# First batch of a fused attention and expert kernel: order of scores and z turns, place of the weight loads, issuer of the tail stores

## The chip, the cores and the metric

The kernel runs on one core of one Trainium2 chip. The metric is the device time of one execution in microseconds (us). The time before is the median of six executions, 1219.36 us, with 1209.82 as the shortest and 1236.12 as the longest.

## The reference

There are 8 batches of 3008 rows. Per batch, with z of 64 columns and u and v of 256:

```
scores = (1/S) * z @ z.T              # 3008 x 3008
attn   = maximum(scores, 0) ** 2
x      = u * (attn @ v)               # 3008 x 256
h      = x @ w_in                     # 256 -> 2048
out    = (h * sigmoid(1.702 * h)) @ w_out   # 2048 -> 256
```

Inputs and output are f32; the kernel works in f16 with f32 sums.

## The kernel before, in words

**Chunks and units.** A batch is cut into six chunks of 512 queries (the last has 448). A chunk has 24 key blocks of 128, and two key blocks make a *unit* (i, jp): two score matmuls of 64 rows (L216), a Relu on ScalarE (`rl`, L228), and a square on VectorE (`a`, L242). Scores are symmetric, so a chunk computes only the units on and behind its diagonal. Units whose key blocks lie in a later chunk are also turned by a DMA transpose from SP's queue (`tt<-a`, L248), and that later chunk multiplies by the turned copy. In batch 0 there are 20 such transposes.

**Attend.** `attend(b, i)` (L270) gives a list of steps for chunk i. A step is one or two matmuls of `V16` with a unit (`o`, L301). In batch 0, chunks 0 and 1 use 128-row matmuls, the later ones 64-row pairs. When a chunk's sum is complete, VectorE multiplies it with the turned u (`xt`, L318). For the 64-row pairs, a nop on POOL stands between the two halves (`post`, L82): it waits for TensorE to reach step 23, and later POOL instructions stand behind it.

**Order.** All engines run in the order in which the program is written; each engine takes its instructions strictly in that order. Tables place the rest of the work by chunk and step: SCHED0 (L570) says at which step how many units are scored (`take`, L581), TURN0 and LOAD0 when u is turned and the next u is loaded, FIRST_ZT (L569) when a chunk of z is turned in chunk 0, LOADW (L566) when W2 is loaded.

**Start of batch 0.** z comes in f32 by DMA. `first_cast(g)` (L120) makes two f16 copies of a 512-row piece on VectorE; `first_zt(g)` (L125) turns the piece with four TensorE transposes into a PSUM tile `zp` and copies it to `ZT` (L134 on ScalarE for piece 0, L136 on VectorE for the others). The copy reads PSUM in order and writes f16 values 8 bytes apart, since a row's four key blocks lie side by side. Warm-up matmuls on zeros (L94) fill TensorE before. In the kernel before, all six pieces are cast ahead of the first three units' squares on VectorE:

```
    warm_up(9)
    first_cast(0); first_zt(0); first_cast(1); first_zt(1)
    for g in range(2, NCH):
        first_cast(g)
    take(0, 2); take(0, 1); load_u(0, 1); first_zt(2); warm_up(2)
```

(written here on fewer lines than in the code). Pieces 3 to 5 are turned at steps 3, 11 and 19 of chunk 0.

**Weights.** W1 (four DMAs, L636) and W2 (four DMAs, L372) are f32 in memory and f16 on the chip, and are loaded from POOL's queue, as u is (L186). W1's first half is issued after chunk 0, its second half after chunk 1, each behind a small copy (`hold`) that waits for that chunk's `xt`. W2 follows in chunk 4. Four VectorE sums over W2 (`weight_sums`, L374) give the right-hand sides of a seven-product scheme.

**Up and down.** `up_group` (L335) computes one 128-column pair of h: four matmuls (`hg`, L342), Gelu on ScalarE (`gf`, L350), a scaling on VectorE (`gt`, L351). The first 20 groups of a batch are laid into chunk 5's steps, one behind each other two or three `o` matmuls; the other 28 alternate with the products of chunks 0 to 3 (`st`, L432). After a chunk's eighth group, each later group carries one more VectorE sum (`left_sum`, L395). The last two chunks go through `down64` (L495), whose matmuls alternate with the first scores of the next batch; it too has POOL nops, at its steps 16 and 32. At its end `store` (L476) issues the output DMA from ScalarE's queue.

Of the kernel before, what the change touches and what calls it, by code (L numbers as in the profile page):

```python
# [11 lines left out]
P = 128  # L12
# [3 lines left out]
def kernel(  # L16
# [75 lines left out]
    def warm_up(n):  # L92

        w = ps1.tile([P, CH], F32, name="w", tag="ps1")  # L94
        for k in range(n):
            pe.matmul(w, nil[:, :P], nil, start=(k == 0), stop=(k == n - 1))
# [23 lines left out]
    def first_cast(g):  # L120
        m = g % CB * CB
        for c in range(2):
            dve.tensor_copy(ZT["st"][g // CB][:, m:m + CB, c, :], ZT["f"][g // CB][:, m:m + CB, :])  # L123

    def first_zt(g):  # L125
        z2 = ZT["st"][g // CB][:, g % CB * CB:(g % CB + 1) * CB]
        zp = ps1.tile([P, CB, P], F16, name="zp", tag="ps1")
        for k in range(CB):
            pe.transpose(zp[:, k, :], z2[:, k, :, :], ident)
        zt = ZT[0][:, g * CB:(g + 1) * CB, :].rearrange("d n p -> d (n p)")  # L130
        nb = CB if g < NCH - 1 else CB - 1
        dst = zt[:, :nb * P].rearrange("d (p n) -> d n p", n=nb)
        if g == 0:
            act.activation(dst, zp[:, :nb, :], AF.Copy, scale=1.0)  # L134
        else:
            dve.tensor_copy(dst, zp[:, :nb, :])  # L136
        if nb < CB:
            dve.tensor_copy(zt[:, nb * P:], zp[:, nb, :])

# [130 lines left out]
    def attend(b, i, both=False):  # L270


        n = width(i)
        js, cs = list(range(NJ - 1)), range(2)
        own = i * CB
        if b == 0 and i == 3:
            js = js[own:-CB + 1] + js[:own] + js[-CB + 1:]
        elif b and i == NCH - 3:
            js = js[own:own + 2] + js[own + CB:-CB + 1] + js[:own] + js[own + 2:own + CB] + js[-CB + 1:]
        elif b and i < NCH - 2:  # L280
            js = js[own:own + 2] + js[own + CB:-CB + 1] + js[own + 2:own + CB] + js[:own] + js[-CB + 1:]
        half = [(0, TOP, NJ - 1), (1, LOW, NJ - 1)]
        if both:
            order = [[(c, FULL, j)] for j in js[:-CB] for c in cs] + [[(c, FULL, j)] for c in cs for j in js[-CB:]]
            order.insert(-CB, half)
        elif i == NCH - 1:
            order = [half] + [[(c, FULL, j)] for c in cs for j in js]
        else:
            order = [[(0, TOP, j), (1, LOW, j)] for j in js] + [half] + [[(1, TOP, j), (0, LOW, j)] for j in js]
        flat = [(k, m) for k, ms in enumerate(order) for m in ms]  # L290
        first = {c: next(m for m in flat if m[1][0] == c) for c in cs}
        final = {c: [m for m in flat if m[1][0] == c][-1] for c in cs}
        acc, turn = {}, NJ if order[-1][0][1] != FULL else -1

        def step(k):
            done = []
            for m in order[k]:
                c, h, j = m
                if (k, m) == first[c]:
                    acc[c] = ps1.tile([P, CH], F32, name="o", tag="ps1")  # L300
                ins = pe.matmul(  # L301
                    acc[c][:, :n], V16[b][h, j, c, :], weights(b, i, j)[h],
                    start=(k, m) == first[c], stop=(k, m) == final[c],
                )
                if k == turn:
                    behind(acc["sig"], ins)
                done.append(ins)
            if k == turn - 1:
                acc["sig"] = post(done)
            for c in cs:  # L310
                if k == final[c][0]:
                    gate(c)

        def gate(c):
            ut = UT[b, i][:, c].rearrange("p q t -> p (q t)")
            x = XT[b, i]
            if i < NCH - 1 or b % 2:
                dve.tensor_tensor(x[:, c, :n], acc[c][:, :n], ut[:, :n], ALU.mult)  # L318
            else:
                dve.tensor_tensor(x[:, c, :LFULL], acc[c][:, :LFULL], ut[:, :LFULL], ALU.mult)  # L320
                dve.tensor_tensor(XT[b + 1, i][:, c, LAST:], acc[c][:, LFULL:n], ut[:, LFULL:n], ALU.mult)

        XT[b, i] = XT.get((b, i)) or pa.tile([P, NCC, CH], F16, name="xt", tag="xt", bufs=6)
        if i == NCH - 1 and b % 2 == 0:
            XT[b + 1, i] = pa.tile([P, NCC, CH], F16, name="xo", tag="xo")
        return [lambda k=k: step(k) for k in range(len(order))]
# [38 lines left out]
    LO, HI = slice(0, NFF // 2), slice(NFF // 2, NFF)  # L365
    C0, C1 = slice(0, P), slice(P, D)

    def load_w2(k):
        hold = const.tile([P, 1], F16, name=f"hold2{k}")
        pool.tensor_copy(hold, XT[0, NCH - 3][:, 0, :1])  # L370
        fs = slice(k * CB, (k + 1) * CB)
        pool.dma_start(W2[:, fs], moe_w_out.rearrange("(fo p) c -> p fo c", p=P)[:, fs])  # L372

    def weight_sums():  # L374
        b11, b12, b21, b22 = W2[:, LO, C0], W2[:, LO, C1], W2[:, HI, C0], W2[:, HI, C1]
# [119 lines left out]
    def down64(b, k):  # L495

        ns = blocks(b)[k][1] // P
        shift, per = (2, 2) if ns == CB else (1, 1)
        order = [(s, (s + shift) % ns, ff) for s in range(ns) for ff in range(NFF)]
        turns = [32] if ns == CB else [16, 32]  # L500
        last = {s // per: n for n, o in enumerate(order) for s in o[:2]}
        yp, sigs = {}, {}

        def step(n):
            s0, s1, ff = order[n]
            done = []
            for s, h in ((s1, LOW), (s0, TOP)):
                new = s // per not in yp
                if new:
                    yp[s // per] = ps1.tile([P, 2, D], F32, name="yp", tag="ps1")  # L510
                ins = pe.matmul(  # L511
                    yp[s // per][:, s % per, :], GT[b, k, ff // CB][h, ff % CB, s * P:(s + 1) * P], W2[h, ff, :],
                    start=new, stop=n == last[s // per],
                )
                if n in turns:
                    behind(sigs[n], ins)
                done.append(ins)
            if n + 1 in turns:
                sigs[n + 1] = post(done)
            for m in yp:  # L520
                if n == last[m]:
                    if (b, k) not in Y:
                        Y[b, k] = pw.tile([P, CB, D], F32, name="y", tag="y")
                    act.activation(Y[b, k][:, m * per:(m + 1) * per, :], yp[m][:, :per, :], AF.Copy, scale=1.0 / FSC)  # L524
            if n == len(order) - 1:
                store(b, k, ns - 1)

        return turns, [lambda n=n: step(n) for n in range(len(order))]

# [33 lines left out]
    TURN0 = {(i, (38, 28)[i] if i < 2 else NJ + 4 if i < NCH - 1 else 12): i for i in range(NCH)}  # L563
    LOAD0 = {(i, n): i + 2 for i, n in TURN0 if i + 2 < NCH}
    TURN = {(1, NJ + 4): 2, (2, NJ + 4): 3, (4, NJ + 4): 4, (5, 8): 5}
    LOADW = {4: 0, 10: 1, NJ + 3: 2, NJ + 9: 3}  # L566
    LOAD = {(3, NJ + 4): 4, (4, NJ + 5): 5}

    FIRST_ZT = {3: 3, 11: 4, 19: NCH - 1}  # L569
# [22 lines left out]
    first_z((0, CB, 2 * CB, 4 * CB, NJ))  # L592
    for n0 in range(VB, NJ, VB):
        load_v(0, n0, sp)
    warm_up(9)
    first_cast(0)
    first_zt(0)
    first_cast(1)
    first_zt(1)
    for g in range(2, NCH):  # L600
        first_cast(g)
    take(0, 2)
    take(0, 1)
    load_u(0, 1)
    first_zt(2)
    warm_up(2)

    for b in range(B):
        nup = NCH * NFG
# [2 lines left out]
        for i in range(NCH):  # L612
            for n, step in enumerate(attend(b, i, b == 0 and i < 2)):
                if b == 0 and i == 0 and n == 5:
                    load_u(0, 0)
                if b == 0 and i == 0 and n in FIRST_ZT:
                    first_zt(FIRST_ZT[n])
                if (i, n) in turn:
                    turn_u(b, turn[i, n])
                if (i, n) in load:  # L620
                    load_u(b, load[i, n])
                if b == 0 and i == NCH - 2 and n in LOADW:
                    load_w2(LOADW[n])
                take(b, sched[i].get(n, 0))
                if i == NCH - 1 and n >= HEAD and (n - HEAD) * LAGY // (2 * NJ - 2 - HEAD) >= head and head < LAGY:
                    up_group(b, head)
                    head += 1
                    if b == 0 and head in (1, 3, 5, 7):
                        weight_sums()[head // 2]()
                step()  # L630
            if b == 0 and i < 2:
                hold = const.tile([P, 1], F16, name=f"hold{i}")
                pool.tensor_copy(hold, XT[b, i][:, 0, :1])
                w1v = moe_w_in.rearrange("(q k c) f -> q c k f", k=NCC, c=QW)
                for k in range(2 * i, 2 * i + 2):
                    pool.dma_start(W1[k * QW:(k + 1) * QW], w1v[k])  # L636
        more = b + 1 < B
        if more:
            for i in range(2):
# [55 lines left out]
```

## Time and profile before

| quantity | value |
|---|---|
| median of 6 executions | 1219.36 us |
| shortest, longest of the 6 | 1209.82, 1236.12 us |
| the profiled execution, its own time | 1236.12 us |
| its span, first to last instruction | 1234.2 us |
| TensorE busy, share of the span | 1200.2 us, 97% |
| VectorE, ScalarE, POOL busy | 823.0, 768.8, 304.1 us |
| mean granted TensorE clock | 0.990 |
| time between chunk 1's end and chunk 2's start on TensorE, idle | 21.7 us |

The profiled execution is the longest of the six. Times inside it are counted from its span's start. `PE` is TensorE's matmuls, `PEld` its weight loads, `DVE` VectorE, `ACT` ScalarE; a `q` behind an engine is its sequencer, which issues DMAs. In a timeline a line gives the start, the length, the engine and line of code, the operation, output and inputs, shapes, how many instructions were merged, and in brackets the idle time before and what ended it. A group of the page gives, after the first bar, busy us and mean ns of one, and after the second bar the idle time and what ended it.

### The profile page before, as it was taken

Reading aid. Unit: us, or ns where it says so; the run is one execution under the profiler, and the core shown is the slowest. Engines: PE = TensorE matmul, PEld = TensorE weight load, DVE = VectorE, ACT = ScalarE, POOL = GpSimd, SP = SyncE. Lnnn points to the kernel's source line nnn. Section 1 sums busy time; section 2 is a strip of 40 time slices with the busy share of each in tenths; the row PEclk is TensorE's granted clock in tenths of the full one; section 3 lists DMA queues with packets and bytes.
Section 4 is the critical chain, followed back from the end, with each engine's and each line's share of the span. In section 5 each row is a group of like instructions: output and inputs, shape, how many; then the busy total and the mean of one; then the engine's idle time right before and its main releaser. Section 6 shows DMA issues by size and latency. Waiting matters only on the chain.

```text
span 1234.2 us, 28037 instructions
## 1 busy us (share of the span) xinstructions
PE 1200.2 (97%) x11691; PEld 720.7 (58%) x11691; DVE 823.0 (67%) x1257; ACT 768.8 (62%) x897; POOL 304.1 (25%) x352
## 2 busy tenths in 40 slices
PE   8489999999999999999999999999999999999998
PEld 3134675547755577445775467644676547855576
DVE  7348976479664895649855498546965479664882
ACT  5348768366773767637675476845768366773773
POOL 4114510055102541025300363003420055101000
PEclk9789999999999999999999999999999999999999
DMA  9985639844497456956379453995439844496012
GB/s 214 98 110 87 152 91 186 135 75 139 120 174 136 64 160 130 180 101 143 99 140 171 91 122 104 167 166 86 134 91 181 145 75 135 133 172 121 1 36 69
DMA packets 370815, 152.32 MB, mean 123 GB/s; under 512 B 313248, under 2 KB 364320, under 8 KB 370688
## 3 DMA queue, kind: packets, MB, share of 16 engines
q1 hardware_dynamic: 328960, 113.16, 48.3%
q0 software_dynamic: 33600, 29.37, 12.7%
q10 hardware_dynamic: 8128, 8.00, 2.1%
q8 instruction: 91, 1.49, 0.5%
q14 instruction: 36, 0.29, 0.1%
HBM read 60.29 MB, written 24.64 MB: 69 GB/s over the span
## 4 chain that ended last, share of the span: by engine, by line
PE 90%; DMA 5%; ACT 2%; DVE 1%; issue 1%; ACTq 0%; SPq 0%; DVEq 0%
PE o L301 36%; PE hg L342 26%; PE st L432 16%; PE yp L511 6%; PE sc L216 5%; DMA tt<-a 4%; ACT rl L228 1%; PE yp L466 1%; ACT y L524 1%; DMA zf<-in_z_dram 0%; DVE zst L123 0%; DVE gt L351 0%; ACTq L484 0%; DVE a L242 0%; ACT gf L350 0%
## 5 line engine op out<-in xcount | busy, mean ns | idle before, releaser
L350 ACT ACTIVATE gf<-hg 128x1024 f32<-128x1024 f32 (+1 forms) x384 | 385.4, 1006 | 166.7 <-PE hg L342 136.6
L228 ACT ACTIVATE rl<-sc 128x1024 f16<-128x1024 f32 x311 | 306.8, 1024 | 235.9 <-PE sc L216 225.1
L301 PEld LDWEIGHTS <-V 64*128 64x128 f16 (+1 forms) x4052 | 237.9, 95 | 272.3 <-DMA tt<-a 25.7
L342 PE MATMUL hg<-xt,W 128*128 128x512 f16 (+1 forms) x1408 | 354.6, 375 | 0.7 <-ACT gf L350 0.5
L351 DVE TENSOR_SCALAR gt<-gf 128x1024 f16<-128x1024 f32 (+1 forms) x384 | 279.4, 728 | 92.3 <-ACT gf L350 88.8
L242 DVE TENSOR_TENSOR a<-rl 128x1024 f16<-128x1024 f16 x276 | 191.8, 696 | 205.2 <-ACT rl L228 203.4
L301 PE MATMUL o<-a,V 64*128 64x512 f16 (+2 forms) x2010 | 319.4, 375 | 1.0 <-DVE a L242 1.0
L186 POOL DMA_DIRECT2D uq<-in_u_dram x188 | 129.4, 695 | 642.3 <-PE sc L216 464.3
L301 PE MATMUL o<-tt,V 64*128 64x512 f16 (+1 forms) x1762 | 216.4, 378 | 23.4 <-DMA tt<-a 23.4
L342 PEld LDWEIGHTS <-W 128*128 128x128 f16 x1536 | 141.1, 98 | 118.4 <-issue 1.4
L432 PEld LDWEIGHTS <-gt 128*128 128x128 f16 x2048 | 125.1, 98 | 28.5
L216 PE MATMUL sc<-ZT 64*128 64x512 f16 (+1 forms) x692 | 123.3, 372 | 1.8 <-DVE zst L123 0.7
L171 POOL CAST V<-vst 128x512 f16<-128x512 f32 x96 | 93.7, 1013 | 64.0 <-DMA vst<-in_v_dram 50.2
L432 PEld LDWEIGHTS <-s 128*128 128x128 f16 x1536 | 93.8, 98 | 21.0
L511 PE MATMUL yp<-W,gt 64*128 64x256 f16 x1664 | 104.0, 270 | 0.0
L511 PEld LDWEIGHTS <-gt 64*128 64x128 f16 x1664 | 80.5, 94 | 19.0 <-POOLq L84 4.0
L318 DVE TENSOR_TENSOR xt<-o,ut 128x512 f16<-128x512 f32 x80 | 51.5, 685 | 38.2 <-PE o L301 38.2
L432 PE MATMUL st<-WT,s 128*128 128x128 f16 x1024 | 67.6, 219 | 0.0
L432 PE MATMUL st<-WT,gt 128*128 128x128 f16 x1024 | 67.6, 220 | 0.0
L432 PE MATMUL st<-W,gt 128*128 128x128 f16 x1024 | 67.6, 219 | 0.0
L216 PEld LDWEIGHTS <-ZT 64*128 64x128 f16 x692 | 38.8, 95 | 41.1 <-issue 10.7
L193 DVE STREAM_TRANSPOSE ut<-uq 128x1024 f32<-128x1024 f32 (+1 forms) x48 | 58.3, 1215 | 0.0
(49 smaller groups left out, 616.8 us busy)
## 6 DMA issues: line engine op xcount, KB each, us to landing
vst<-in_v_dram SPq DMA_DIRECT2D x39, 512.0 KB, 4.7
uq<-in_u_dram POOLq DMA_DIRECT2D x156, 128.0 KB, 3.3
out_dram<-y SPq DMA_DIRECT2D x32, 512.0 KB, 3.8
out_dram<-y ACTq DMA_DIRECT2D x8, 512.0 KB, 4.1
tt<-a SPq DMA_TRANSPOSE x230, 3.6
uq<-in_u_dram POOLq DMA_DIRECT2D x32, 112.0 KB, 2.9
vst<-in_v_dram SPq DMA_DIRECT2D x8, 384.0 KB, 4.7
out_dram<-y ACTq DMA_DIRECT2D x7, 384.0 KB, 5.0
```

Of the source, the lines that this page charges most:

```text
L171: pool.tensor_copy(V16[b][:, n0:n0 + VB, k, :].rearrange("p n (q c) -> p n q c", c=QW), vst.rearrange("p n (q k c) -> p n q k c", k=NCC, c ...
L186: eng.dma_start(uq[k * QW:(k + 1) * QW, :n // QW].rearrange("t q k c -> t q (k c)"), src[:, :, cs])
L193: dve.transpose(ut[:, :, :n // QW, :].rearrange("p k q t -> p q k t"), UQ.pop((b, i))[:, :n // QW])
L216: pe.matmul(sc[:, r, :m * P], zt[h, 2 * kp + r, :], zt[h, (qi + 1) * CB - m:(qi + 1) * CB, :], start=True, stop=True,)
L228: act.activation(rl, sc, AF.Relu, scale=csc)
L242: dve.tensor_tensor(a, rl, rl, ALU.mult)
L301: ins = pe.matmul(acc[c][:, :n], V16[b][h, j, c, :], weights(b, i, j)[h], start=(k, m) == first[c], stop=(k, m) == final[c],)
L342: pe.matmul(hg[:, e, :n], W1[:, c, ff * P:(ff + 1) * P], XT[b, i][:, c, :n], start=(c == 0), stop=(c == NCC - 1),)
L350: act.activation(gf[:, :, :n], hg[:, :, :n], AF.Gelu_apprx_sigmoid, scale=1.0 / FSC)
L351: dve.tensor_scalar(g, gf[:, :, :n], FSC, None, ALU.mult)
L432: pe.matmul(bank[:, m, :], lhs()[:, f, m, :], right[:, ff, :], start=name in ("P1", "P2", "P5") and m == 0 and ff == 0, stop=ff == NFF // ...
L511: ins = pe.matmul(yp[s // per][:, s % per, :], GT[b, k, ff // CB][h, ff % CB, s * P:(s + 1) * P], W2[h, ff, :], start=new, stop=n == last[ ...
```

## The change

The change has five parts. The copy out of `zp` reads PSUM with a stride and writes `ZT` in order. In the prologue the units 0 and 1 are scored ahead of piece 1's turn, unit 2 ahead of piece 2's cast, and the casts of pieces 3 to 5 move to steps 3, 11 and 19 of chunk 0, each directly ahead of its turn; the warm-up matmuls are split 7, 3 and 2. Chunk 4 of batch 0 takes its own key blocks first, as chunk 3 did. All eight weight loads go through one function, placed at chunk 3, steps 25 and 35 (W1), chunk 4, steps 2 and 10 (W1), and chunk 5, steps 0 to 18 (W2); the four sums over W2 move from heads 1 to 7 to heads 13 to 19 of chunk 5. `down64`'s store is issued from POOL.

```diff
@@ first_zt
-        dst = zt[:, :nb * P].rearrange("d (p n) -> d n p", n=nb)
+        dst = zt[:, :nb * P].rearrange("d (p n) -> d p n", n=nb)
+        src = zp[:, :nb, :].rearrange("d n p -> d p n")
         if g == 0:
-            act.activation(dst, zp[:, :nb, :], AF.Copy, scale=1.0)
+            act.activation(dst, src, AF.Copy, scale=1.0)
         else:
-            dve.tensor_copy(dst, zp[:, :nb, :])
+            dve.tensor_copy(dst, src)
@@ attend
-        if b == 0 and i == 3:
+        if b == 0 and i in (3, 4):
             js = js[own:-CB + 1] + js[:own] + js[-CB + 1:]
@@ loads
-    def load_w2(k):
-        hold = const.tile([P, 1], F16, name=f"hold2{k}")
-        pool.tensor_copy(hold, XT[0, NCH - 3][:, 0, :1])
-        fs = slice(k * CB, (k + 1) * CB)
-        pool.dma_start(W2[:, fs], moe_w_out.rearrange("(fo p) c -> p fo c", p=P)[:, fs])
+    def load_w(k):
+        if k == 0:
+            hold = const.tile([P, 1], F16, name="hold")
+            pool.tensor_copy(hold, XT[0, 1][:, 0, :1])
+        if k < 4:
+            w1v = moe_w_in.rearrange("(q k c) f -> q c k f", k=NCC, c=QW)
+            pool.dma_start(W1[k * QW:(k + 1) * QW], w1v[k])
+        else:
+            fs = slice((k - 4) * CB, (k - 3) * CB)
+            pool.dma_start(W2[:, fs], moe_w_out.rearrange("(fo p) c -> p fo c", p=P)[:, fs])
@@ down64
-                store(b, k, ns - 1)
+                store(b, k, ns - 1, pool)
@@ tables
-    LOADW = {4: 0, 10: 1, NJ + 3: 2, NJ + 9: 3}
+    LOADW = {(3, NJ + 1): 0, (3, NJ + 11): 1, (4, 2): 2, (4, 10): 3, (5, 0): 4, (5, 6): 5, (5, 12): 6, (5, 18): 7}
@@ prologue
-    warm_up(9)
+    warm_up(7)
     first_cast(0)
     first_zt(0)
+    warm_up(3)
     first_cast(1)
+    take(0, 2)
     first_zt(1)
-    for g in range(2, NCH):
-        first_cast(g)
-    take(0, 2)
+    warm_up(2)
     take(0, 1)
     load_u(0, 1)
+    first_cast(2)
     first_zt(2)
-    warm_up(2)
@@ main loop
                 if b == 0 and i == 0 and n in FIRST_ZT:
+                    first_cast(FIRST_ZT[n])
                     first_zt(FIRST_ZT[n])
...
-                if b == 0 and i == NCH - 2 and n in LOADW:
-                    load_w2(LOADW[n])
+                if b == 0 and (i, n) in LOADW:
+                    load_w(LOADW[i, n])
...
-                    if b == 0 and head in (1, 3, 5, 7):
-                        weight_sums()[head // 2]()
+                    if b == 0 and head in (13, 15, 17, 19):
+                        weight_sums()[head // 2 - 6]()
                 step()
-            if b == 0 and i < 2:
-                hold = const.tile([P, 1], F16, name=f"hold{i}")
-                pool.tensor_copy(hold, XT[b, i][:, 0, :1])
-                w1v = moe_w_in.rearrange("(q k c) f -> q c k f", k=NCC, c=QW)
-                for k in range(2 * i, 2 * i + 2):
-                    pool.dma_start(W1[k * QW:(k + 1) * QW], w1v[k])
```

## The prediction

> **What bounds the kernel now.** I read the page's first and fifth parts, then the waits of the first 200 us, the timelines of TensorE, VectorE and POOL there, and the DMA view in stretches. TensorE is busy 97% of the span, and after 190 us its idle time sums to about 3 us, so the seven later batches are bound by matmul work that the change doesn't touch. What can move lies before 200 us. From the waits:
>
> ```profile
> PE o L301 <- DMA tt<-a: 21.7, 1, 21.7
> PE zp L129 <- DVE zst L123: 1.1, 1, 1.1
> PE o L301 <- DVE a L242: 1.0, 1, 1.0
> PE sc L216 <- DVE zst L123: 0.7, 1, 0.7
> PE hg L342 <- ACT gf L350: 0.5, 1, 0.5
> ```
>
> One wait, on a transposed unit, is 21.7 of the 28.7 us that TensorE idles. TensorE's timeline, at the start and around it:
>
> ```profile
> 12.53 1.44 PE L301 MATMUL o<-a,V 128*128 128x512 f16 x3 [0.96 <-DVE a L242]
> 13.76 0.64 PE L129 MATMUL zp<-ident,zst 128*128 128x128 f16 x4
> ...
> 18.03 0.39 PE L129 MATMUL zp<-ident,zst 128*128 128x128 f16 x4
> ...
> 20.63 0.39 PE L129 MATMUL zp<-ident,zst 128*128 128x128 f16 x4
> ...
> 66.57 1.46 PE L301 MATMUL o<-tt,V 64*128 64x512 f16 x6 [21.70 <-DMA tt<-a]
> ```
>
> The first `o` starts at 12.53; the turns at steps 3, 11 and 19 start at 13.76, 18.03 and 20.63 without a wait. The DMA view of 28 to 67 us:
>
> ```profile
> uq<-in_u_dram POOLq DMA_DIRECT2D x8, 128.0 KB, 16.0
> W<-in_moe_w_in_dram POOLq DMA_DIRECT2D x4, 256.0 KB, 19.0
> tt<-a SPq DMA_TRANSPOSE x8, 14.2
> ```
>
> and of 67 to 92 us, after W1 has landed:
>
> ```profile
> tt<-a SPq DMA_TRANSPOSE x8, 4.3
> ```
>
> The last column is us from issue to landing: eight transposes took 14.2 us with W1 in the queues and 4.3 after it. In 44 to 60 us the engines moved only about 100 GB/s. POOL's timeline has the W1 issues:
>
> ```profile
> 31.30 1.08 POOL L636 DMA_DIRECT2D W<-in_moe_w_in_dram  x2
> ...
> 44.60 1.08 POOL L636 DMA_DIRECT2D W<-in_moe_w_in_dram  x2
> ```
>
> The first pair came 1.7 and 8.2 us ahead of the two transposes that chunk 2 needs last (SP issued them at 32.96 and 39.53; they landed at 55.6 and 66.5), and nothing reads W1 before the first `hg` at 104.7.
>
> **What the Trainium skill says.** "DMA: Bandwidth & Descriptors", Queues, rings and completion order: every DMA engine takes its queues in turn, a packet at a time, so POOL's and SP's transfers share it. The trace agrees (14.2 against 4.3 us). "TensorE: Matmul & The Clock Gate", What's actually happening: after an idle window of some 3.4 us TensorE falls to half clock until it has been busy for a window. The trace agrees: 128x512 matmuls start 0.43 us apart until 17.4 us and 0.216 after, and 66.6 to 72.0 runs at half clock again. "Vector Engine (DVE) Microarchitecture Reference", Measured stream behaviour on trn2: a stream that hops at every element costs 1.7 to 2.5 ns a column instead of 1.05, on the reading side as on the writing side. The trace has the hopping write (512 columns in 1.29 us) and an ordered copy (128 in 0.20); no row has a hopping PSUM read.
>
> **Part 1, W1 and W2 moved: -24.4 us in the profiled execution.** With W1 gone, 28 to 67 us holds two u loads (1 MB) beside the transposes instead of 2 MB. That u alone is harmless is seen at 20 to 28 us (eight u loads, transposes 6.4 to 7.1 us) and in the later batches (transposes 3.5 us median, 7.4 at most). The two units that chunk 2 waits for are squared by about 32 us; at 7 us they land by 40, ahead of 44.5. So the 21.7 us go, and with them the half clock of 66.6 to 72.0, half of 5.4 or 2.7 us. The new place: POOL issues W1's first part behind chunk 3's nop (step 23, 86.5 us), its other three behind the last u load of batch 0 (90.8), about 0.55 us each. A 128 KB u load landed in 2.9 there; four W1 parts should be in by 100, ahead of 104.7. W2 goes behind chunk 4's nop (98.4): 4 issues of 0.75, landings of 4.2 to 5.4 us, and some 2 us of all engines for each, so in by about 109; head 13 comes at about 122. No transposes run between 87 and 123. Behind these issues on POOL stand only the next batch's u, z and v, not needed before 130.
>
> **Part 2, the start: +6.0 us (bounds +4 and +9).** In the new order VectorE casts piece 2 behind unit 2's square, and pieces 3, 4, 5 behind the squares of the units scored at steps 0, 6 and 14. TensorE takes its queue in order, so each turn now waits for a chain score, Relu, square, cast. Durations from the timelines: score to Relu 0.65 cold, 0.43 warm; Relu 1.02, a second one 0.92 later; square 0.69; the two casts 0.74; hand-overs 0.05.
> First `o`: turn of piece 0 at 4.4 (two warm-ups fewer), its ScalarE copy 5.05 to 5.7 or 6.4, third warm-up ends 6.1, so score 0 at 6.1 to 6.4; Relus 0 and 1 end by 8.7 to 9.0, square 1 by 9.4 to 9.8, piece 1's copy (0.65 to 1.3) by 10.1 to 11.1, score 2, Relu (+1.7), square (+0.7), cast of piece 2 (+0.75): 13.3 to 14.3; turn and score 3, 0.43 each: first `o` at 14.1 to 15.1 against 12.53. The old block of eight casts,
>
> ```profile
> 8.51 2.96 DVE L123 CAST zst<-zf 128x256 f16<-128x256 f32 x8
> ```
>
> is gone from in front of square 0, but square 0 isn't what the first `o` waits for any more.
> Step 3: score 3 at 13.7 to 14.7, +0.65+1.02+0.69+0.74+0.1, so the turn at 16.9 to 17.9 against 13.76; three `o` end 1.5 us earlier. Step 11: turn (0.22 or 0.43), three `o` (0.65 or 1.28), then two scores, whose chain is 0.5+0.92+1.02+0.69+0.74+0.1 = 4.0: the turn at 21.7 to 23.7 against 18.03. Step 19 likewise: 26.5 to 29.5 against 20.63. That is +5.9 to +8.9. Casts after 17 us no longer share time with POOL's casts, and half-clock matmuls in the waits are hidden, where before they were not (some 2 us); so I take +6.0. Faster copies save little: copies 2 to 5 lie outside these chains, and the +4 end is a copy and Relu at their best. From step 19 on TensorE is dense in both, so nothing is won back. Chunk 4's own-first order adds no matmul and its own units are squared in chunk 3's first half: 0.
>
> **Part 3, sums over W2 later: +1.2 us (0 to +2.4).** At heads 9 to 20 VectorE has two operations of 0.605 us per group, TensorE 1.28 us per group; it was already late:
>
> ```profile
> 125.99 1.02 PE L342 MATMUL hg<-xt,W 128*128 128x512 f16 x4 [0.52 <-ACT gf L350]
> ```
>
> Four sums of 0.605 are 2.4 us, taken from heads 1 to 7, where VectorE had gaps, into this stretch. Two buffers of `hg` and of `gf` let it fall about 1.5 us behind; half of 2.4 is my value. Behind head 20 a group lasts 1.75 us on TensorE and the lag dissolves.
>
> **Part 4, tail stores from POOL: -0.5 us (-1.5 to +1.5).** ScalarE loses 14 issues like this:
>
> ```profile
> 187.11 1.08 ACT L524 ACTIVATE y<-yp 128x512 f32<-128x512 f32 x2
> 188.23 0.39 ACTq L484 DMA_DIRECT2D out_dram<-y  x1
> ```
>
> TensorE's waits for Relus at the batch changes sum to 1.1 us, so that is what can be had. Against it: on POOL the store waits for `y` (188.2) and takes 0.55 (64-row stores) to 1.0 us; behind it stands the nop that TensorE needs from 189.07 on. In four of seven changes that is 0 to 0.3 us late; whoever waits then is `yp`, then the first scores.
>
> **Sum.** 1236.1 - 24.4 + 6.0 + 1.2 - 0.5 = 1218.4 us. This is against the profiled execution, the longest of six. Elsewhere TensorE has 7 us of idle time in all, so the median execution can only be 17 us shorter through a shorter stall: without any, the sum gives 1211.7, and the shortest execution is 1209.82. The median thus has some 8 us of stall to lose, and the start costs about as much.
>
> **Rivals.** (a) The start costs much more, as TensorE's gaps keep it at half clock until about 30 us: each cycle between turns becomes 5.8 instead of 4.6 us, and the offset 9 to 13: 1222 to 1231. For it: no window between 13 and 27 us is free of gaps; against it: most of the half-rate work hides in the waits. (b) The start costs at most 2 us, because the chain is shorter than I add up or the old start was worse than it looks: 1204 to 1213. For it: first scores come 1.0 us earlier; against it: the in-order waits above. (c) Slower: the transposes stay late, since the u loads alone hold them up. The place is the tenth transpose; it decides when it lands after TensorE reaches chunk 2 (about 50 us in the new order). Price: up to 21.7 + 2.7, so 1228 to 1243. For it: u loads share the slow stretch (16.0 us); against it: u with transposes at 20 to 28 us and in every later batch. (d) The change doesn't do what it says, POOL running ahead to the W1 issues: excluded by chunk 3's nop in front of them; within (c).
>
> **Chances.** Main case 0.55 (its own range 1213 to 1224), (a) 0.16, (b) 0.18, (c) 0.11. One per cent, about what a measurement of this kernel can tell from no change, is 1207.2 to 1231.6. Under it fall 0.11 out of (b). Over it fall 0.03 of (a) and 0.07 of (c). So faster 0.11, same 0.79, slower 0.10. The range of 1206 to 1231 leaves out about a tenth on each side.
>
> **What would show it.** Right: no `tt<-a` wait over 1 us ahead of chunk 2, transposes landing in under 8 us; first `o` near 14.5; turns (`zp`) behind `zst` waits of about 1.5, 2 and 2 us; the last turn near 27; `hg` waits of 1 to 2 us about the new 125; no new waits on POOL's nops over 0.3. Wrong: turns without waits, a `tt<-a` wait that stays, `hg` waiting for W1, or an `st` for the W2 sums.

## The result, and the profile after

The changed kernel takes 1218.58 us (median of 34 runs, 1215.24 to 1221.68). The kernel before, run beside it and its variants 71 times, takes 1215.62 us (1207.74 to 1236.12). The ratio is 1.0028, with a 95% interval of 1.0015 to 1.0041: slower by some 3 us, where the forecast was 1218.4 us and about 1 us faster. The time was met and the direction was not, because the kernel before is faster than the median of its first six runs, and because the new start costs more than was forecast. The medians here and below are of all executions; the ratios leave out those more than 1.5% above the fastest of their kernel.

The profiled execution of the changed kernel has a span of 1216.1 us (before: 1234.2) and took 1217.83 us (before: 1236.1). TensorE's longest waits in the first 200 us of the changed kernel (us in total, times, longest):

```profile
PE zp L129 <- DVE zst L123: 7.9, 4, 3.1
PE sc L217 <- DVE ZT L137: 2.2, 1, 2.2
...
PE hg L343 <- ACT gf L351: 0.8, 2, 0.4
```

The 21.7 us wait on a transposed unit is gone. In its place stand 7.9 us in which turns of z (`zp`) wait for casts, and 2.2 us in which a score waits for the copy of piece 1. TensorE's timeline shows where (start, busy us, and in brackets the idle time before and who ended it):

```profile
10.10 0.39 PE L217 MATMUL sc<-ZT 64*128 64x512 f16 x2 [2.18 <-DVE ZT L137]
13.63 0.61 PE L129 MATMUL zp<-ident,zst 128*128 128x128 f16 x4 [3.15 <-DVE zst L123]
...
14.71 1.46 PE L302 MATMUL o<-a,V 128*128 128x512 f16 x3
17.69 0.61 PE L129 MATMUL zp<-ident,zst 128*128 128x128 f16 x4 [1.51 <-DVE zst L123]
...
23.28 0.40 PE L129 MATMUL zp<-ident,zst 128*128 128x128 f16 x4 [1.47 <-DVE zst L123]
...
27.82 0.40 PE L129 MATMUL zp<-ident,zst 128*128 128x128 f16 x4 [1.77 <-DVE zst L123]
```

The first `o` starts at 14.71 against 12.53, and the turns at steps 3, 11 and 19 start at 17.69, 23.28 and 27.82 against 13.76, 18.03 and 20.63. VectorE's timeline shows what each turn waits for:

```profile
15.88 0.94 DVE L243 TENSOR_TENSOR a<-rl 128x1024 f16<-128x1024 f16 x1 [0.91 <-ACT rl L229]
16.74 0.89 DVE L123 CAST zst<-zf 128x256 f16<-128x256 f32 x2
```

VectorE stands idle for 0.91 us until a Relu comes, squares it, and casts only then: the cast, which needs nothing but z, is queued behind a chain that starts on TensorE itself. The DMA view of 28 to 67 us, where W1 no longer loads, shows why the long wait is gone (last column: us from issue to landing; before, u took 16.0 and the transposes 14.2):

```profile
uq<-in_u_dram POOLq DMA_DIRECT2D x12, 128.0 KB, 3.2
tt<-a SPq DMA_TRANSPOSE x16, 3.4
```

Part of the 3.4 us is the slower start, which spreads the transposes: with the old start, and with u as the only load beside them, the transposes took 6.4 and 5.9 us (28 to 52 us; the kernels with the weights alone and with the start undone, below). From 67 to 92 us W1 and W2 load now:

```profile
W<-in_moe_w_in_dram POOLq DMA_DIRECT2D x4, 256.0 KB, 4.4
W<-in_moe_w_out_dram POOLq DMA_DIRECT2D x4, 256.0 KB, 5.8
```

W1 has landed by 82.5 us, and the first `hg` runs at 87.36 without waiting for it. The two spans (1234.2 and 1216.1) can be split at places that both have:

| stretch | before, us | after, us | difference |
|---|---|---|---|
| start to chunk 0's two half-row matmuls, 1.3 us before its end | 27.84 | 35.04 | +7.2 |
| to the first `hg` | 76.84 | 52.32 | -24.5 |
| to the first `yp` | 74.04 | 75.13 | +1.1 |
| to the end | 1055.5 | 1053.6 | -1.9 |

The last row, to which the tail stores belong, varies between 1053.2 and 1057.0 over the ten profiles whatever the kernel, so its -1.9 says nothing.

### The profile page after: what moved, and what is told of

It is laid out like the page before. It is cut to its first block, busy times and chain, and to the rows that moved or that the text cites. A ratio compares the mean times of both kernels' runs of the same rounds, so it can differ in the third digit from the quotient of the medians.

```text
span 1216.1 us, 28032 instructions
## 1 busy us (share of the span) xinstructions
PE 1196.4 (98%) x11692; PEld 715.0 (59%) x11692; DVE 819.0 (67%) x1257; ACT 768.5 (63%) x897; POOL 309.1 (25%) x361
## 4 chain that ended last, share of the span: by engine, by line
PE 95%; DVE 2%; DMA 1%; ACT 1%; issue 0%; ACTq 0%; DVEq 0%
PE o L302 37%; PE hg L343 26%; PE st L439 16%; PE yp L518 8%; PE sc L217 6%; DMA tt<-a 1%; PE yp L473 1%; ACT rl L229 1%; DVE gt L352 1%; PE w L96 0%; DVE a L243 0%; DVE zst L123 0%; PE zp L129 0%; DVE s L410 0%; ACT gf L351 0%
## 5 line engine op out<-in xcount | busy, mean ns | idle before, releaser
L302 PEld LDWEIGHTS <-V 64*128 64x128 f16 (+1 forms) x4052 | 233.0, 95 | 253.0 <-issue 10.7
L352 DVE TENSOR_SCALAR gt<-gf 128x1024 f16<-128x1024 f32 (+1 forms) x384 | 275.1, 717 | 94.4 <-ACT gf L351 91.1
L172 POOL CAST V<-vst 128x512 f16<-128x512 f32 x96 | 90.0, 974 | 66.2 <-DMA vst<-in_v_dram 66.0
L152 POOL COPY zst<-zst 128x768 f16<-128x768 f16 x14 | 45.2, 3231 | 53.9 <-DMA zst<-in_z_dram 53.9
```

Source lines behind the costliest of these rows:

```text
L172: pool.tensor_copy(V16[b][:, n0:n0 + VB, k, :].rearrange("p n (q c) -> p n q c", c=QW), vst.rearrange("p n (q k c) -> p n q k c", k=NCC, c ...
L302: ins = pe.matmul(acc[c][:, :n], V16[b][h, j, c, :], weights(b, i, j)[h], start=(k, m) == first[c], stop=(k, m) == final[c],)
L352: dve.tensor_scalar(g, gf[:, :, :n], FSC, None, ALU.mult)
```

## The experiments

The theory after the result: the profiled execution of before had a far longer stall than the usual run; moving the weights takes away a usual stall of 5 to 8 us, and the new start gives more than that back. The variants were run in two groups, beside which the kernel before took 1216.58 us (the weights alone, the start alone, the old start, all casts behind two squares) and 1216.17 us (the others), against 1215.62 above; so a difference between medians of different groups is good to about 1 us. The rivals: (A) the weights cost in their new place, (B) the late sums or the stores on POOL eat the gain, and (C) the u loads alone keep the transposes late.

**One part alone.** The kernel before with the weight part only (`load_w`, the new `LOADW`, the sums at heads 13 to 19, chunk 4's own-first order):

```diff
...
-    LOADW = {4: 0, 10: 1, NJ + 3: 2, NJ + 9: 3}
+    LOADW = {(3, NJ + 1): 0, (3, NJ + 11): 1, (4, 2): 2, (4, 10): 3, (5, 0): 4, (5, 6): 5, (5, 12): 6, (5, 18): 7}
...
```

> The kernel before with only the later weight loads, the later sums over W2 and chunk 4's own-first order; start, copies and stores as before. Theory (the W1 loads make the transposes late, the new start costs 7 us): no wait on tt<-a ahead of chunk 2, the four sums cost about 1 us, 1211 us (1209.5 to 1212.5), and runs that differ by far less than those of before. Rival A (the time of the changed kernel is lost through the late weights, sums or stores, and the start is hidden): 1216 to 1219 us. Rival B (the u loads make the transposes late): a tt<-a wait of 5 us or more stays ahead of chunk 2.

Measured: 1210.07 us, ratio 0.9952 (0.9936 to 0.9969), and a spread of only 1208.01 to 1212.49 where before ran from 1208.52 to 1232.28 beside it. No wait for a transposed unit is left ahead of chunk 2. So the weight part is a gain of some 6.5 us at the median, its new place does not take it back (rival A falls), and with the stall most of the scatter of the kernel before is gone.

The kernel before with the start only (score units ahead of casts and turns, and the new copy):

```diff
...
-    warm_up(9)
+    warm_up(7)
     first_cast(0)
     first_zt(0)
+    warm_up(3)
     first_cast(1)
+    take(0, 2)
     first_zt(1)
-    for g in range(2, NCH):
-        first_cast(g)
-    take(0, 2)
+    warm_up(2)
     take(0, 1)
     load_u(0, 1)
+    first_cast(2)
     first_zt(2)
-    warm_up(2)
...
+                    first_cast(FIRST_ZT[n])
                     first_zt(FIRST_ZT[n])
```

> The kernel before with only the new start and the new copy; weight loads, sums and stores as before. Theory: the turns at steps 3, 11 and 19 wait 1.5 to 1.8 us each and the first o is near 14.7, about 7 us on top of the median of before: 1222 to 1224 us, with the wide spread of before since W1 still meets the transposes. Rival A: within 2 us of before. A third possibility, that the slower start spreads the transposes and so takes part of the stall away: 1217 to 1221 us with a tt<-a wait under 3 us.

Measured: 1219.39 us, ratio 1.0033 (1.0013 to 1.0053), and its profile has no wait on a transposed unit although W1 is loaded early. The last two transposes that chunk 2 needs landed at 48.9 and 49.8 us, and TensorE came to chunk 2 at about 50.8: the slower start lets them through, by about 1 us in this profile. Some runs of it still reach 1232 us. So the two cures overlap, and in a 2 by 2 table of medians they don't add (1218.58 is the changed kernel, which has the stores on POOL as well):

| | weights early | weights late |
|---|---|---|
| old start | about 1216 | 1210.07 |
| new start | 1219.39 | 1218.58 |

**Undo the start.** The changed kernel with before's order of casts, turns and score units, everything else kept, the new copy too:

> The changed kernel with the old start (nine warm-ups, all casts ahead of the first squares); copy, weight loads, sums and stores as changed. Theory: turns at steps 3, 11, 19 without waits, 1210 us (1208.5 to 1211.5), 8 us under the changed kernel. Rival A: 1217 to 1219 us.

Measured: 1209.56 us, ratio 0.9941 (0.9918 to 0.9964). The order of the start alone costs 1218.58 - 1209.56 = 9.0 us. Against the weights-only kernel, which has before's copy and stores as well, the difference is 1218.58 - 1210.07 = 8.5 us. The profiles of the changed kernel and of this one divide it. Chunk 1 first multiplies a turned unit at 36.9 us against 25.3, so 11.6 us later (25.3 is the earliest of three profiles with this start and copy; the others have 26.1 and 27.5). Of these, 4.5 us lie ahead of the first `o` (14.71 against 10.17), 4.8 are the three waits for casts behind it, and the 2.3 that are left are slower matmuls: TensorE's granted clock is at half from 10.4 to 20.7 us in the changed kernel, and at full from 6.1 us on in this one. Three `o` matmuls show it, first in the changed kernel, then in this one:

```profile
18.09 1.49 PE L302 MATMUL o<-a,V 128*128 128x512 f16 x3
```

```profile
11.04 0.81 PE L302 MATMUL o<-a,V 128*128 128x512 f16 x3
```

It is not this one pair of profiles alone: the mean granted clock is 0.9951 over the runs of the changed kernel and 0.9980 over the 22 of this one, which is some 7 us more at half clock (an estimate from these means).

**How usual is the stall.** The kernel before once more, for a second profile:

> The kernel before, once more, for a profile of a usual execution. Theory: its wait on tt<-a ahead of chunk 2 is about its time less 1209 us, so 5 to 10 us for 1214 to 1219 us, with W1 landing 10 to 20 us after its issue. Rival (the difference to the profiled execution lies elsewhere): a wait of some 20 us again at a time of about 1216.

Measured: 1215.48 us. The stall is there, at a quarter of its first length, in TensorE's timeline (these six matmuls take 0.81 us at full clock, at 41.89 us of the same profile):

```profile
48.44 1.46 PE L301 MATMUL o<-tt,V 64*128 64x512 f16 x6 [5.31 <-DMA tt<-a]
```

and in the DMA view of 28 to 52 us the same loads and transposes landed faster than in the first profile (19.0 and 14.2, in 28 to 67 us):

```profile
W<-in_moe_w_in_dram POOLq DMA_DIRECT2D x4, 256.0 KB, 9.3
...
tt<-a SPq DMA_TRANSPOSE x8, 9.9
```

TensorE's clock comes back to full at 53.3 us, so behind the wait 4.9 us of matmuls run at half clock, which costs 2.4 us more. 1215.48 less 5.3 and 2.4 is 1207.8, and the shortest of the 71 executions of before is 1207.74. Between the two profiles of before, whose spans differ by 20.7 us, the stall makes up 16.4. So it is the stall that sets most of its time from run to run. Not all scatter comes from it: the changed kernel with the old start ran from 1205.81 to 1218.30 us with its weights late, which is left open.

**Which cast costs what.** The changed kernel with casts 3, 4 and 5 one place earlier, ahead of the squares that they stood behind:

```diff
-                    first_cast(FIRST_ZT[n])
                     first_zt(FIRST_ZT[n])
...
+                if b == 0 and i == 0 and n in (0, 6, 14):
+                    first_cast({0: 3, 6: 4, 14: NCH - 1}[n])
                 take(b, sched[i].get(n, 0))
```

> The changed kernel with one thing moved: the casts of pieces 3, 4 and 5 stand on VectorE ahead of the squares of the units scored at steps 0, 6 and 14 instead of behind them. Theory (each turn waits for score, Relu and square because its cast is queued behind them): the waits on zst at steps 3, 11 and 19 (1.51, 1.47, 1.77 us) fall under 0.5 us each, those for piece 1's copy and piece 2's cast (2.2 and 3.2 us) stay, 1213.5 us (1212 to 1215). Rival (the turns are late because TensorE is at half clock or VectorE is full): 1217 to 1219 us and waits that stay.

Measured: 1213.46 us, ratio 0.9986 (0.9959 to 1.0012), 5.1 us better than the changed kernel, where 5 were expected. Its waits of the first 80 us, and its turns at steps 3, 11 and 19 in TensorE's timeline:

```profile
PE zp L129 <- DVE zst L123: 3.5, 1, 3.5
PE sc L217 <- DVE ZT L137: 2.4, 1, 2.4
```

```profile
16.20 0.63 PE L129 MATMUL zp<-ident,zst 128*128 128x128 f16 x4
...
20.44 0.39 PE L129 MATMUL zp<-ident,zst 128*128 128x128 f16 x4
...
23.03 0.39 PE L129 MATMUL zp<-ident,zst 128*128 128x128 f16 x4
```

Three of the four waits for casts are gone, with no bracket left at any of the three turns, and 7.9 us have become 3.5. So 5.1 of the 9 us are these three turns. The other 4 were not undone one by one. This profile has no wait between the first `o` and chunk 1, and against the profile with the old start it differs in two things: the first `o` is 4.8 us later (14.94 against 10.17), as piece 1's copy stands behind two squares and the cast of piece 2 behind a third, and from there to chunk 1's first turned unit TensorE takes 17.1 us instead of 15.1, at half clock until 19.7. That is 6.8 us and not 4; this profile's execution (1216.47 us) lies 3 us above its kernel's median, the other's 1.2 below.

The other way round, the changed kernel with the score units still first but all four casts in one block behind piece 1's copy:

```diff
...
+    for g in range(2, NCH):
+        first_cast(g)
     warm_up(2)
     take(0, 1)
     load_u(0, 1)
-    first_cast(2)
     first_zt(2)
...
-                    first_cast(FIRST_ZT[n])
```

> The changed kernel, but with the casts of pieces 2 to 5 all behind the squares of units 0 and 1 and piece 1's copy, ahead of unit 2's square. Theory: the first o starts near 11.5, as it waits only for squares 0 and 1 and for piece 2's turn; step 3's turn no longer waits for a chain of its own; 1209 us (1207.5 to 1210.5), 1 us under the changed kernel with the old start. Rival A: 1216 to 1219 us.

Measured: 1210.96 us, ratio 0.9962 (0.9942 to 0.9981). It wins 7.6 of the 9 us, but a gain of 1 us over the old start was expected and its median is 1.4 us behind it (the intervals of the two ratios overlap, so that it is slower is not shown); the first `o` came at 11.97 us instead of the expected 11.5 (old start with the new copy: 10.17). Two reasons are seen. A score still waits for the copy behind two squares, and the block itself got slower. VectorE's timeline has it, first in this kernel, then in the one with the old start:

```profile
9.96 3.74 DVE L123 CAST zst<-zf 128x256 f16<-128x256 f32 x8
```

```profile
7.83 1.70 DVE L123 CAST zst<-zf 128x256 f16<-128x256 f32 x8
```

POOL's timeline has its casts of V, again in this kernel and then with the old start:

```profile
9.32 1.17 POOL L172 CAST V<-vst 128x512 f16<-128x512 f32 x2 [2.82 <-DMA vst<-in_v_dram]
```

```profile
9.45 7.08 POOL L172 CAST V<-vst 128x512 f16<-128x512 f32 x7 [2.86 <-DMA vst<-in_v_dram]
```

The block that ends about where they begin takes 1.70 us and the one that lies beside them 3.74; between the two are 2.14, 2.55 and 2.96 us (starts at 8.22, 8.15 and 8.51 in three profiles with before's copy). The place in the order is not the cause: in the kernel with casts 3 to 5 moved, two casts took 1.31 us beside a cast on POOL (at 12.49) and 0.48 us while POOL stood idle (at 15.12). So scoring first shows no gain in this start even with the casts together.

**The stores and the sums.** With the old start, the tail stores given back to ScalarE:

```diff
-                store(b, k, ns - 1, pool)
+                store(b, k, ns - 1)
```

> The changed kernel with the old start and the tail stores back on ScalarE. Theory of the prediction (stores from POOL gain about 0.5 us): 1210 us, 0.5 over the same kernel with stores from POOL (1209.56). Rival (stores from POOL meet the next batch's first transposes on the DMA engines and give the gain back; tt<-a waits of TensorE after the first batch were 4.0 and 4.4 us in two kernels with stores from POOL and 0.7 and 1.8 in two with stores from ScalarE): 1209 us or less, and tt<-a waits under 2 us behind 190 us.

Measured: 1209.02 us, ratio 0.9943 (0.9925 to 0.996), against 1209.56 with POOL: not told apart. The waits behind 190 us do differ. First the changed kernel's, then this one's:

```profile
PE o L302 <- DMA tt<-a: 2.1, 4, 1.5
```

```profile
PE o L302 <- DMA tt<-a: 1.3, 3, 0.5
PE sc L217 <- ACT rl L229: 0.4, 1, 0.4
```

With the stores on POOL this view has no wait for a Relu in any of the four profiles that have them so (0.4 to 1.7 us in the six with ScalarE), and the waits for transposed units are 2.1, 4.0, 4.4 and 5.3 us (0 to 1.8 with ScalarE). So in these profiles the transposes take back what the Relus gave; why the stores on POOL make them late was not tested.

Then, on top of it, W2's four loads at the start of chunk 5 and the sums at heads 5 to 8, where the aim was to win back the 1.1 us between the first `hg` and the first `yp`:

```diff
...
-    ... (5, 0): 4, (5, 6): 5, (5, 12): 6, (5, 18): 7}
+    ... (5, 0): 4, (5, 1): 5, (5, 2): 6, (5, 3): 7}
...
-                    if b == 0 and head in (13, 15, 17, 19):
-                        weight_sums()[head // 2 - 6]()
+                    if b == 0 and head in (5, 6, 7, 8):
+                        weight_sums()[head - 5]()
```

> The changed kernel with the old start, the tail stores back on ScalarE and the four sums over W2 at heads 5 to 8 of chunk 5 (W2's four issues follow one another at steps 0 to 3). Theory: the sums fill VectorE's gaps there and the 1.1 us that they cost later (first hg to first yp, 75.1 in the changed kernel and 74.0 before) goes; 1208.5 us (1207 to 1210), 1 us under the kernel that only has the stores back. Rival: W2 is not in at head 5 and VectorE waits, with no gain or a loss.

Measured: 1207.1 us, ratio 0.9942 (0.9922 to 0.9962): the fastest median here. But its profile has 75.12 us from the first `hg` to the first `yp`, like every kernel with the sums at heads 13 to 19; in its timeline VectorE's gaps lie ahead of head 5, up to 87.8 us, and from there on the sums, a turn of u and the left sums fill it without one. Its median is 1.9 us below that of the kernel that it builds on, but the two ratios, against the same runs of before, are the same (0.9942 and 0.9943), so that lead is open and no cause is claimed for it. The waits of its first 200 us also have something new:

```profile
PE o L302 <- DMA tt<-a: 2.4, 1, 2.4
```

No weight is in the queues then; in 28 to 52 us only u loads (5.8 us to landing) share them with the transposes (6.0). So rival C has a small part: with the early start and u alone, a transpose can still be 2 us late. It is not so each time: the three other profiles with the early start and late weights have no such wait ahead of chunk 2.

## Why the prediction was right and wrong

**Against the profiled execution the sum held, in part by luck.** It went from 1236.1 to 1218.4; the table by stretches ends 18.1 us lower on the spans and the executions differ by 18.3, against 17.7 forecast. Part 1 was -24.4 and the stretch gave -24.5. Part 3 was +1.2 and the stretch gave +1.1, though of the `hg` waits of 1 to 2 us only two of 0.4 us are seen as waits. The `hg` waited for no weight, and no `st` for a sum. (The u load of 2.9 us by which W1's landing was judged has 112 KB and not 128; W1's parts landed 3.8 to 5.4 us after issue, early enough all the same.) But the start was +7.2 in that table where +6.0 was forecast, and what made up for it is the last row's -1.9, which says nothing.

**The places of the start held.** First `o` forecast at 14.1 to 15.1, seen at 14.71; turns at 16.9 to 17.9, 21.7 to 23.7 and 26.5 to 29.5, seen at 17.69, 23.28 and 27.82; waits of about 1.5, 2 and 2 us, seen as 1.51, 1.47 and 1.77.

**The step that failed is the cost of the start, +6.0 us, which the last sentence of the sum sets against the stall: "The median thus has some 8 us of stall to lose, and the start costs about as much."** Undoing the start gives 9.0 us, the upper bound that the prediction itself had added up. It took 6.0, near the low end of +5.9 to +8.9, for two savings of some 2 us. The first was casts that no longer share time with POOL's. The old block, 2.96 us in the first profile, took only 2.14 and 2.55 us in the two later profiles with that start and copy, so there was less to save. The second, half-clock work hidden in waits "where before they were not", took the start of the first profile for the usual one. There TensorE runs at half clock until 17.4 us. In the two later profiles it comes to full clock at 5.5 and 5.3 us and falls back to half from 8.9 to 12.3 and from 8.8 to 15.6; in the changed kernel it comes to full at 7.0 and is at half again from 10.4 to 20.7. So the new start has more half-clock work than the usual old one. The last turn shows the same: before's first profile has it at 20.63 us, the two later ones at 18.89 and 19.24, and against these the changed kernel's 27.82 is 8.6 to 8.9 us later, not 7.2.

The stall was sized about right. The second profile has 5.3 + 2.4 = 7.7 us of it, and the weights alone won 6.5 us (1216.58 to 1210.07) with the later sums, of about 1.1, already paid. But both ends of the 8 us were too high: 1219.36 against a median of 1215.62 over 71 runs, and 1211.7 without a stall against 1207.8. Then 9.0 - 6.5 is +2.5 us, where +3.0 was measured. That 1218.4 and 1218.58 agree is luck: a time without a stall that was 3.9 us too high stood against a start that was 3 us too cheap.

**A case that was not listed.** The sum took the parts one by one. The start-only kernel shows that a later start by itself removes most of the stall, so that with it the move of the weights, with the later sums and the stores on POOL, is worth only 1219.39 - 1218.58 = 0.8 us, which these medians don't tell from nothing, and a narrower spread.

**Rivals.** (a), a start that costs 9 to 13 us, was right in its size only at its low edge. Its cause had a part: TensorE is at half clock until 20.7 us, not until about 30, and that makes some 2 us; the larger part is the chain to the first `o` and the three waits. (b), a cheap start, fell. (c), u alone, was seen only in one of the kernels with the early start, with 2.4 us. (d) fell: W1 was issued from 69.8 us on. **Part 4** named the waits that it would remove, and they went; it didn't foresee that waits on transposed units would come instead. Its net lies within what the runs can tell.

## What to carry to other kernels

Before an operation is put later in an in-order queue, count what stands between it and the engine that waits for it: a cast that needed only loaded data became the end of score, Relu, square, cast, and cost 5.1 us at three places until it was moved ahead of those squares. A stall that varies from run to run has to be sized over many runs, not from the profile that happens to show it, which here was the longest of the first six; the same holds for what is to be saved elsewhere, as this profile had a late start too. Two edits that cure one stall are to be costed together, since a slower stage ahead of it is a cure as well. Where a bundle of edits comes out near zero, undo each: here one part was worth 6.5 us and another cost 9.

## What was not expected of the hardware

**Strided PSUM reads cost nothing that these profiles show.** The Trainium skill, "Vector Engine (DVE) Microarchitecture Reference", Measured stream behaviour on trn2, prices a hopping read like a hopping write, for 4-byte words; it has no row for a read of PSUM, and the forecast left the copy at 0.65 to 1.3 us. The new copy writes in order and reads PSUM with hops, in ScalarE's timeline and in VectorE's:

```profile
4.95 0.60 ACT L135 ACTIVATE ZT<-zp 128x512 f16<-128x512 f16 x1 [2.40 <-PE zp L129]
```

```profile
14.28 0.69 DVE L137 COPY ZT<-zp 128x512 f16<-128x512 f16 x1 [0.70 <-PE zp L129]
```

In the kernel before, with ordered reads and hopping writes, they took twice as long:

```profile
5.68 1.31 ACT L134 ACTIVATE ZT<-zp 128x512 f16<-128x512 f16 x1 [3.15 <-PE zp L129]
```

```profile
14.02 1.29 DVE L136 COPY ZT<-zp 128x512 f16<-128x512 f16 x1
```

So for this f16 copy the measurement decides: the hop costs on the writing side and not on the reading side. With the old start this brings casts ahead of POOL's (first `o` at 10.17 us against 11.35 with the old copy), though the medians, 1209.02 and 1210.07 with ScalarE's stores in both, don't separate it.

**Casts on VectorE slow down beside casts on POOL**: eight took 1.70 us in front of POOL's casts of V and 3.74 beside them, and two in one and the same profile 0.48 and 1.31 us.

**Transposes beside POOL's loads vary from run to run** in the same program: eight with W1 in the queues landed in 14.2 us (median) in one profile of the kernel before and in 9.9 in another, and the stall that followed was 21.7 and 5.3 us. Why one run is so much worse is left open.
